# Layer 0's weight conversion in half steps: a spectral layer and two MLPs on one Trainium2 core

## The chip, the cores and the metric

The kernel runs on one core of one Trainium2 chip. The metric is the device time of one execution in microseconds (us), from the first to the last instruction and what lies around them; lower is better.

## What is computed

Two batches of 3008 x 256 go through a real Fourier transform along the sequence, a complex 256 x 256 linear map with a bias and a soft threshold, and the transform back. The 6016 x 256 result passes two MLPs of width 2048, one with a PReLU (`alpha`), one with a quadratic gate. Cut to what matters:

```
X = rfft(x, axis=1)
Yr, Yi = Xr @ w_r - Xi @ w_i + b_r,  Xr @ w_i + Xi @ w_r + b_i
Y = sign(Y) * max(|Y| - 0.01, 0)        (both parts)
x = irfft(Y).reshape(6016, 256)
h = x @ w_in;   x = (max(h,0) + alpha*min(h,0)) @ w_out           # layer 0
h = x @ w_in2;  out = where(h>=1, h, where(h<=-1, 0, (h+1)**2/4)) @ w_out2   # layer 1
```

The MLP weights reach the kernel as float64 words, read as pairs of 32-bit integers; the kernel itself makes an fp32r pair of high and low part from each.

## The kernel before

**Phases.** Phase 1 (`f1`) makes the first factor of the transform. Phase 2 runs over 24 items `(b, i)`, 12 per batch, in passes j = 0 to 23. Pass j emits `f2(j+2)` (second factor for the item two ahead), `mix(j)` (the complex map), `i1(j-2)` (first factor back), from pass 16 on `p3(j-16)` (second factor back, which yields the MLP's input `y`), and then steps of the weight conversion. Passes 22 and 23 have no `f2` left. Behind the loop stand `i1` of item 22, the first MLP block `first(0, 0, 0)`, and `i1` of item 23. Then come the MLPs: 12 chunks of tokens times 16 blocks f of the hidden width for each of two layers. Step i emits `first` of one block and `second` of the block three steps earlier; the first two chunks are interleaved in 32 steps.

**Order.** The schedule is manual: each engine works through its instructions in the order in which the code emits them. SP (SyncE) issues nearly all DMAs, also in that order. So an instruction that waits holds back all that stands behind it on its engine.

**An item of phase 2.** ACT (ScalarE) copies the PSUM of `f2` to the high half `fh` (lines 317, 318), DVE (VectorE) subtracts for the low half `fl` (319), ACT completes it (320); only then can `mix` use the item. Behind `mix`, DVE makes `t`, `clip` and `y` (337 to 339), and `i1` needs `y`. PSUM has four buffers under each of two tags: `mix` and `i1` share "o", all the rest "h".

**The conversion.** Block f of layer 0 is loaded by two DMAs to staging buffer `u` (three of them, taken in turn), and then goes through this sequence; `cm` and `cp` have two buffers each:

- ACT 145 `cm<-u` (absolute value of the top word), ACT 146 `u<-u` (the low word as a float), DVE 147 `cp<-u` (the sign)
- DVE 179 clamp of `cm`, DVE 158 `cm<-cm,cp`, which finishes the value
- ACT 174 `w<-cm`, the high part of the weight; DVE 163 and 164, the fraction of the low word
- DVE 168 `cm<-cm,w` and 169 `w<-cm,cp`, the low part

The generator `conversions` yields after each step. Before, a step is either "163, 164, 174 of block k-1 and 145 to 147 of block k" or "168, 169 of block k-1, then 179, 158 of block k, then the load of block k+2". So a block takes two steps. In passes 5 to 16 one step is taken, in passes 17 to 21 two, in 22 and 23 one; in the interleaved chunks one at each step i that 3 does not divide. Layer 1's first 15 blocks use GpSimd (E is G) and keep their steps.

Of the kernel before, what the change touches and what calls it, by code (L numbers as in the profile page):

```python
# [74 lines left out]
def spectral_mlp_kernel(ctx: ExitStack, tc: tile.TileContext, x, w_r, w_i, bias, c_f1, c_f2,  # L75
# [47 lines left out]
    def in_place(l, f):  # L123
        return l == 1 and f >= 12
# [9 lines left out]
        nc.sync.dma_start(u[:, 256:512, :].rearrange("p m z -> p (m z)"),  # L134
                          w_dram[l][1][f * 128:(f + 1) * 128, :].bitcast(U32))

    def convert_w(l, f, part, clamp, low_engine):
        E = low_engine
        if part == 0:
            u = stage.pop((l, f))  # L140
            m = rot.tile([128, 512], F32, tag="cm", name=f"cm{l}_{f}")
            p = rot.tile([128, 512], F32, tag="cp", name=f"cp{l}_{f}")
            live[l, f] = u, m, p
            top, low = u[:, :, 1], u[:, :, 0]
            A.activation(m, top.bitcast(F32), AF.Abs, scale=2.0 ** -16)
            A.activation(low.bitcast(F32), low, AF.Copy, scale=2.0 ** -52)
            V.tensor_scalar(p.bitcast(U32), top, 0x80000000, 0x80000000, op0=ALU.bitwise_and, op1=ALU.bitwise_xor)
            if clamp is G:
                clamp_w(l, f, G)
            return  # L150
        u, m, p = live[l, f]
        low = u[:, :, 0].bitcast(F32)
        mu, pu = m.bitcast(U32), p.bitcast(U32)
        if part == 1:
            if clamp is V:
                clamp_w(l, f, V)

            V.scalar_tensor_tensor(mu, mu, 3, pu, op0=ALU.logical_shift_left, op1=ALU.bitwise_xor)
        elif part == 2:
            if not in_place(l, f):  # L160
                high_w(l, f, m)

            V.tensor_scalar(pu, mu, 0xFF800000, None, op0=ALU.bitwise_and)
            E.tensor_tensor(p, p, low, op=ALU.mult)
        else:
            if in_place(l, f):
                high_w(l, f, m)
            E.tensor_tensor(m, m, wt[l, f][:, 0, :].bitcast(F32), op=ALU.subtract)
            E.tensor_tensor(wt[l, f][:, 1, :], m, p, op=ALU.add)
            del live[l, f]  # L170

    def high_w(l, f, m):
        wt[l, f] = block(w_tag[l, f], [128, 2, 512], F32R, f"w{l}_{f}")
        A.activation(wt[l, f][:, 0, :], m, AF.Copy)

    def clamp_w(l, f, engine):

        m = live[l, f][1]
        engine.tensor_scalar(m, m, W_MAX, W_MIN, op0=ALU.min, op1=ALU.max)

    def conversions(l, fs, clamp, low_engine):

        n = len(fs)
        for f in fs[:2]:
            load_w(l, f)
            yield
        for k in range(n + 1):
            if k >= 1:
                convert_w(l, fs[k - 1], 2, clamp, low_engine)
            if k < n:  # L190
                convert_w(l, fs[k], 0, clamp, low_engine)
            yield
            if k >= 1:
                convert_w(l, fs[k - 1], 3, clamp, low_engine)
            if k < n:
                convert_w(l, fs[k], 1, clamp, low_engine)
            if k + 2 < n:
                load_w(l, fs[k + 2])
            yield
# [90 lines left out]
    load_a(0, A_PARTS[4:])  # L290
    load_mn(1, n_t, c_i1)
    load_mn(2, m_t, c_f2)
    conv = conversions(0, list(range(NF)), V, V)
    next(conv)
    wm = [block(f"c{k}", [128, 2, 2, D], F32R, f"wm{k}") for k in range(2)]
    for g in range(8, 16):
# [196 lines left out]
    for j in range(n):  # L493
        if 0 < j < n - 2:
            f2(*items[j + 2])
        mix(*items[j])
        if j == 0:
            f2(*items[2])
        if j >= 2:
            i1(*items[j - 2])  # L500

        if j == 3:
            for g in range(8, 16):
                store_a(g, 1)
        if j == 5:
            load_a(1, A_PARTS[:3])
            load_mn(2, n_t, c_i1, 0)
            load_a(1, A_PARTS[3:4])
            load_mn(2, n_t, c_i1, 1)
        if j == 7:  # L510
            load_a(1, A_PARTS[4:])
            nc.sync.dma_start(nalpha, alpha)
            nc.sync.dma_start(g47, c_i2)
        if j == 13:
            for g in range(3):
                load_v(g)
        if j >= P3_AT:
            g = j - P3_AT
            p3(g)
            if g + 3 < 8:  # L520
                load_v(g + 3)
        if j == 20:
            V.tensor_scalar(nalpha, nalpha, -1.0, None, op0=ALU.mult)
        if j == n - 2:
            prep(0, 0)
        for _ in range((j >= 5 or j == 2) + (17 <= j < 22)):
            next(conv)
    i1(*items[n - 2])
    first(0, 0, 0, None)
# [9 lines left out]
    for i in range(len(seq) + DEPTH):  # L539
        if i < len(seq):  # L540
            l, c, f = seq[i]
            if (l, c, f) == (0, 2, 0):
                for _ in conv:
                    pass
                conv = conversions(1, list(range(15)), G, G)
            if (l, c, f) == (0, NC - 1, 4):
                for _ in conv:
                    pass
                conv = conversions(1, [15], V, V)
            if i >= 1:  # L550
                first(l, c, f, seq[i - 1])
            if i == 2:
                prep(0, 1)
            if 8 <= i < 24 and i % 2 == 0:
                p3(4 + i // 2)
            if 3 <= i < 2 * NF and i % 3 != 0 or l == 0 and c >= 2 and f % (2 if c == NC - 1 else 4) == 0:
                next(conv, None)
            if (l, c, f) == (0, 0, NF - 1):
                prep(0, 2)
# [38 lines left out]
```

## Time and profile before

| | |
|---|---|
| median of 3 runs | 1146.31 us (1145.3 to 1146.49) |
| profiled execution | 1149.25 us, span 1147.2 us |
| mean granted TensorE clock | 0.997 |
| PE busy | 1136.1 us, 99% of the span |
| DVE busy | 905.6 us, 79% |
| ACT busy | 630.6 us, 55% |
| phase 2 | about 34 to 154 us of the span |
| MLP layer 0, then 1 | about 155 to 654 us, then to the end |

PE is TensorE's matmul queue. A busy PE is not a PE at its peak, since ends of matmuls are modelled; idle PE time and the granted clock are the safer readings. A wait is named by line and tile: "PE psi L346 <- DVE y L339" is the transform back waiting for the thresholded item.

### The profile page before, as it was taken

The page shows a single profiled execution, that of the slowest core. Times are in us where ns is not written, and L with a number is a line of the kernel's source. Part 1 is how long each engine was busy: PE and PEld are TensorE (multiplying, and loading weights), DVE is VectorE, ACT ScalarE, POOL GpSimd, SP SyncE. Part 2 cuts the span into 40 slices and gives each one's busy share as a digit, 9 for nine tenths or more (in the row PEclk, how much of TensorE's full clock was granted, in tenths as well). Part 3 has the DMA queues.
Part 4 walks back from the last instruction along what each step waited for, and adds up shares of the span by engine and source line. Part 5 has one row for each costly group of instructions (what it writes and reads, how often), then busy time and mean ns, then how long its engine had stood idle before and what let it go on. Part 6 is the DMA issues. An engine that isn't in the chain of part 4 may idle for free.

```text
span 1147.2 us, 17412 instructions
## 1 busy us (share of the span) xinstructions
PE 1136.1 (99%) x6630; PEld 1013.4 (88%) x6630; DVE 905.6 (79%) x1409; ACT 630.6 (55%) x1131; POOL 81.5 (7%) x64
## 2 busy tenths in 40 slices
PE   9999999999999999999999999999999999999998
PEld 6999978888888998888889988888889988888898
DVE  2679977668999999999986777777777777777776
ACT  3455677675655666565555755445445544544553
POOL 0000000000231313212210000000000000000000
PEclk9999999999999999999999999999999999999999
DMA  9997662100010101000000000000000000000000
GB/s 278 323 293 217 183 180 60 57 1 1 20 37 20 37 19 32 25 19 19 1 1 19 1 1 19 19 1 19 19 1 19 17 10 10 20 19 1 19 19 17
DMA packets 38195, 59.40 MB, mean 52 GB/s; under 512 B 3712, under 2 KB 25568, under 8 KB 38112
## 3 DMA queue, kind: packets, MB, share of 16 engines
q1 hardware_dynamic: 37856, 58.14, 16.4%
q8 instruction: 53, 0.87, 0.3%
q14 instruction: 30, 0.25, 0.1%
q10 hardware_dynamic: 256, 0.15, 0.0%
HBM read 39.53 MB, written 18.74 MB: 51 GB/s over the span
## 4 chain that ended last, share of the span: by engine, by line
PE 90%; DVE 4%; DMA 2%; ACT 2%; issue 1%; SPq 0%; DVEq 0%; ACTq 0%
PE pso L95 14%; PE pso L94 14%; PE pso L96 13%; PE psh L94 13%; PE psh L95 13%; PE psh L96 13%; PE psm L332 5%; PE psf L312 2%; PE psi L346 2%; DMA x<-in_x 1%; PE ps L420 1%; DVE gl L91 1%; DVE ta L456 1%; DMA wm<-in_w_r 1%; DMA a_dr<-ae 1%
## 5 line engine op out<-in xcount | busy, mean ns | idle before, releaser
L91 DVE TENSOR_TENSOR gl<-ta,gh 128x512 fp32r<-128x512 f32 (+1 forms) x384 | 274.5, 715 | 50.0 <-ACT gh L88 44.9
L94 PE MATMUL psh<-mxh,w 128*128 128x512 f32 (+1 forms) x768 | 288.9, 376 | 0.7 <-ACT tb L454 0.6
L94 PE MATMUL pso<-gh,w 128*128 128x512 f32 (+1 forms) x768 | 288.5, 376 | 0.0
L95 PE MATMUL psh<-mxl,w 128*128 128x512 f32 (+1 forms) x768 | 288.3, 375 | 0.0
L95 PE MATMUL pso<-gl,w 128*128 128x512 f32 (+1 forms) x768 | 288.0, 375 | 0.2
L96 PE MATMUL psh<-mxh,w 128*128 128x512 f32 (+1 forms) x768 | 288.1, 375 | 0.0
L96 PE MATMUL pso<-gh,w 128*128 128x512 f32 (+1 forms) x768 | 287.7, 375 | 0.0
L461 ACT ACTIVATE ta<-psh 128x512 f32<-128x512 f32 (+1 forms) x192 | 113.6, 592 | 243.5 <-PE psh L96 216.8
L462 DVE SCALAR_TENSOR_TENSOR tb<-ta 128x512 f32<-128x512 f32 (+1 forms) x192 | 130.7, 681 | 116.4 <-ACT ta L461 115.8
L453 ACT ACTIVATE ta<-psh 128x512 f32<-128x512 f32 (+1 forms) x192 | 113.6, 592 | 193.6 <-DVE gl L91 96.6
L456 DVE SCALAR_TENSOR_TENSOR ta<-ta,nalpha,tb 128x512 f32<-128x512 f32 (+1 forms) x192 | 168.0, 875 | 11.9 <-ACT tb L454 11.6
L94 PEld LDWEIGHTS psh<-mxh,w 128*128 128x128 f32 x768 | 145.6, 190 | 18.9 <-ACT tb L454 1.5
L95 PEld LDWEIGHTS psh<-mxl,w 128*128 128x128 f32 x768 | 145.4, 189 | 17.8 <-DVE mxl L91 0.3
L95 PEld LDWEIGHTS pso<-gl,w 128*128 128x128 f32 x768 | 145.1, 189 | 18.1 <-DVE gl L91 1.3
L96 PEld LDWEIGHTS psh<-mxh,w 128*128 128x128 f32 x768 | 145.4, 189 | 17.3
L94 PEld LDWEIGHTS pso<-gh,w 128*128 128x128 f32 x768 | 145.1, 189 | 17.4
L96 PEld LDWEIGHTS pso<-gh,w 128*128 128x128 f32 x768 | 145.2, 189 | 17.2
L88 ACT ACTIVATE gh<-ta 128x512 fp32r<-128x512 f32 (+1 forms) x240 | 147.6, 615 | 1.3 <-DVE ta L464 1.3
L464 DVE TENSOR_TENSOR ta<-psh,tb 128x512 f32<-128x512 f32 (+1 forms) x192 | 129.1, 672 | 0.0
L454 ACT ACTIVATE tb<-psh 128x512 f32<-128x512 f32 (+1 forms) x192 | 112.5, 586 | 0.0
L90 DVE CAST gh<-ta 128x512 fp32r<-128x512 f32 (+1 forms) x144 | 67.1, 466 | 15.2 <-DVE ta L456 0.5
L332 PE MATMUL psm<-wm,fh 128*128 128x256 f32 x384 | 60.6, 280 | 0.0
(54 smaller groups left out, 798.1 us busy)
## 6 DMA issues: line engine op xcount, KB each, us to landing
u<-in_w_in SPq DMA_DIRECT2D x32, 256.0 KB, 2.7
u<-in_w_out SPq DMA_DIRECT2D x32, 256.0 KB, 3.0
v_dr<-ve SPq DMA_DIRECT2D x12, 512.0 KB, 3.1
v<-v_dr SPq DMA_DIRECT2D x32, 192.0 KB, 4.8
x<-in_x SPq DMA_DIRECT2D x15, 384.0 KB, 7.7
out<-yt SPq DMA_DIRECT2D x20, 256.0 KB, 2.0
a<-a_dr SPq DMA_DIRECT2D x6, 768.0 KB, 7.0
a_dr<-ae SPq DMA_DIRECT2D x20, 192.0 KB, 6.6
```

The source lines that it names most:

```text
L88: A.activation(hi, src, AF.Copy)
L91: V.tensor_tensor(lo, src, hi.bitcast(F32), op=ALU.subtract)
L94: T.matmul(ps, wl, xh, start=start, stop=False)
L95: T.matmul(ps, wh, xl, start=False, stop=False)
L96: T.matmul(ps, wh, xh, start=False, stop=stop)
L332: T.matmul(o, x[:, 2 * k + c, off:off + 128], wm[r][:, z, c, :].rearrange("p (h q) -> p q h", h=2), start=n == c == 0, stop=n == 5 and c == 1)
L453: A.activation(ta, ps, AF.Relu, scale=-1.0)
L454: A.activation(tb, ps, AF.Relu)
L456: V.scalar_tensor_tensor(ta, ta, nalpha[:, f:f + 1], tb, op0=ALU.mult, op1=ALU.add)
L461: A.activation(ta, ps, AF.Relu, bias=0.5, scale=0.5)
L462: V.scalar_tensor_tensor(tb, ta, 1.0, ta, op0=ALU.min, op1=ALU.mult)
L464: V.tensor_tensor(ta, ps, tb, op=ALU.max)
```

## The change

The two kinds of step of layer 0 become four: "fraction of block k-1 (174, 163, 164), and 145 of block k", "146 and 147 of block k", "168 and 169 of block k-1", and "179, 158 of block k and the load of block k+2". They are taken twice as often: two in each of passes 5 to 16, four in 17 to 21, none in 22 and 23, one at each step i from 3 in the interleaved chunks. Layer 1's last block, converted beside chunk 11, also takes the small steps, one per block f. No instruction is added or removed.

```diff
--- before.py
+++ after.py
@@ -134,40 +134,39 @@
         nc.sync.dma_start(u[:, 256:512, :].rearrange("p m z -> p (m z)"),
                           w_dram[l][1][f * 128:(f + 1) * 128, :].bitcast(U32))
 
-    def convert_w(l, f, part, clamp, low_engine):
-        E = low_engine
-        if part == 0:
-            u = stage.pop((l, f))
-            m = rot.tile([128, 512], F32, tag="cm", name=f"cm{l}_{f}")
-            p = rot.tile([128, 512], F32, tag="cp", name=f"cp{l}_{f}")
-            live[l, f] = u, m, p
-            top, low = u[:, :, 1], u[:, :, 0]
-            A.activation(m, top.bitcast(F32), AF.Abs, scale=2.0 ** -16)
-            A.activation(low.bitcast(F32), low, AF.Copy, scale=2.0 ** -52)
-            V.tensor_scalar(p.bitcast(U32), top, 0x80000000, 0x80000000, op0=ALU.bitwise_and, op1=ALU.bitwise_xor)
-            if clamp is G:
-                clamp_w(l, f, G)
-            return
+
+    def begin_w(l, f):
+        u = stage.pop((l, f))
+        m = rot.tile([128, 512], F32, tag="cm", name=f"cm{l}_{f}")
+        p = rot.tile([128, 512], F32, tag="cp", name=f"cp{l}_{f}")
+        live[l, f] = u, m, p
+        A.activation(m, u[:, :, 1].bitcast(F32), AF.Abs, scale=2.0 ** -16)
+
+    def words_w(l, f):
         u, m, p = live[l, f]
-        low = u[:, :, 0].bitcast(F32)
-        mu, pu = m.bitcast(U32), p.bitcast(U32)
-        if part == 1:
-            if clamp is V:
-                clamp_w(l, f, V)
-
-            V.scalar_tensor_tensor(mu, mu, 3, pu, op0=ALU.logical_shift_left, op1=ALU.bitwise_xor)
-        elif part == 2:
-            if not in_place(l, f):
-                high_w(l, f, m)
-
-            V.tensor_scalar(pu, mu, 0xFF800000, None, op0=ALU.bitwise_and)
-            E.tensor_tensor(p, p, low, op=ALU.mult)
-        else:
-            if in_place(l, f):
-                high_w(l, f, m)
-            E.tensor_tensor(m, m, wt[l, f][:, 0, :].bitcast(F32), op=ALU.subtract)
-            E.tensor_tensor(wt[l, f][:, 1, :], m, p, op=ALU.add)
-            del live[l, f]
+        top, low = u[:, :, 1], u[:, :, 0]
+        A.activation(low.bitcast(F32), low, AF.Copy, scale=2.0 ** -52)
+        V.tensor_scalar(p.bitcast(U32), top, 0x80000000, 0x80000000, op0=ALU.bitwise_and, op1=ALU.bitwise_xor)
+
+    def sign_w(l, f):
+
+        mu, pu = (t.bitcast(U32) for t in live[l, f][1:])
+        V.scalar_tensor_tensor(mu, mu, 3, pu, op0=ALU.logical_shift_left, op1=ALU.bitwise_xor)
+
+    def fraction_w(l, f, E):
+
+        u, m, p = live[l, f]
+        if not in_place(l, f):
+            high_w(l, f, m)
+        V.tensor_scalar(p.bitcast(U32), m.bitcast(U32), 0xFF800000, None, op0=ALU.bitwise_and)
+        E.tensor_tensor(p, p, u[:, :, 0].bitcast(F32), op=ALU.mult)
+
+    def low_w(l, f, E):
+        u, m, p = live.pop((l, f))
+        if in_place(l, f):
+            high_w(l, f, m)
+        E.tensor_tensor(m, m, wt[l, f][:, 0, :].bitcast(F32), op=ALU.subtract)
+        E.tensor_tensor(wt[l, f][:, 1, :], m, p, op=ALU.add)
 
     def high_w(l, f, m):
         wt[l, f] = block(w_tag[l, f], [128, 2, 512], F32R, f"w{l}_{f}")
@@ -178,7 +177,7 @@
         m = live[l, f][1]
         engine.tensor_scalar(m, m, W_MAX, W_MIN, op0=ALU.min, op1=ALU.max)
 
-    def conversions(l, fs, clamp, low_engine):
+    def conversions(l, fs, E):
 
         n = len(fs)
         for f in fs[:2]:
@@ -186,14 +185,23 @@
             yield
         for k in range(n + 1):
             if k >= 1:
-                convert_w(l, fs[k - 1], 2, clamp, low_engine)
+                fraction_w(l, fs[k - 1], E)
             if k < n:
-                convert_w(l, fs[k], 0, clamp, low_engine)
+                begin_w(l, fs[k])
+                if E is V:
+                    yield
+                words_w(l, fs[k])
+                if E is G:
+                    clamp_w(l, fs[k], G)
             yield
             if k >= 1:
-                convert_w(l, fs[k - 1], 3, clamp, low_engine)
+                low_w(l, fs[k - 1], E)
+                if E is V:
+                    yield
             if k < n:
-                convert_w(l, fs[k], 1, clamp, low_engine)
+                if E is V:
+                    clamp_w(l, fs[k], V)
+                sign_w(l, fs[k])
             if k + 2 < n:
                 load_w(l, fs[k + 2])
             yield
@@ -290,7 +298,7 @@
     load_a(0, A_PARTS[4:])
     load_mn(1, n_t, c_i1)
     load_mn(2, m_t, c_f2)
-    conv = conversions(0, list(range(NF)), V, V)
+    conv = conversions(0, list(range(NF)), V)
     next(conv)
     wm = [block(f"c{k}", [128, 2, 2, D], F32R, f"wm{k}") for k in range(2)]
     for g in range(8, 16):
@@ -523,7 +531,8 @@
             V.tensor_scalar(nalpha, nalpha, -1.0, None, op0=ALU.mult)
         if j == n - 2:
             prep(0, 0)
-        for _ in range((j >= 5 or j == 2) + (17 <= j < 22)):
+
+        for _ in range(j == 2 or (2 if 5 <= j < n - 2 else 0) + (2 if 17 <= j < 22 else 0)):
             next(conv)
     i1(*items[n - 2])
     first(0, 0, 0, None)
@@ -542,18 +551,18 @@
             if (l, c, f) == (0, 2, 0):
                 for _ in conv:
                     pass
-                conv = conversions(1, list(range(15)), G, G)
+                conv = conversions(1, list(range(15)), G)
             if (l, c, f) == (0, NC - 1, 4):
                 for _ in conv:
                     pass
-                conv = conversions(1, [15], V, V)
+                conv = conversions(1, [15], V)
             if i >= 1:
                 first(l, c, f, seq[i - 1])
             if i == 2:
                 prep(0, 1)
             if 8 <= i < 24 and i % 2 == 0:
                 p3(4 + i // 2)
-            if 3 <= i < 2 * NF and i % 3 != 0 or l == 0 and c >= 2 and f % (2 if c == NC - 1 else 4) == 0:
+            if 3 <= i < 2 * NF or l == 0 and c >= 2 and f % (1 if c == NC - 1 else 4) == 0:
                 next(conv, None)
             if (l, c, f) == (0, 0, NF - 1):
                 prep(0, 2)
```

The generator starts with two loads and, for k = 0, with three small steps in place of two large ones. So the pairs fall anew on the passes. Three places follow, with the kernel before ahead of the change; lines in the changed file are 8 higher from 310 on (317 is 325) and 174, 145, 146 are 173, 143, 148; 147, 163, 164, 179, 158 are 149, 161, 162, 178, 154. In names, `fh0_11` is item 11, `fh1_9` is item 12 + 9 = 21, and `cm0_2` is block 2 of layer 0.

ACT around pass 9, before:

```order
L317 ACTIVATE fh0_11_804<-psf0_11_799 128x4x128
L318 ACTIVATE fh0_11_804<-psf0_11_799 128x4x64
L320 ACTIVATE fl0_11_805<-fl0_11_805 128x4x64
L349 ACTIVATE ve0_6_790<-psi0_7_841 128x512
L174 ACTIVATE w0_1_846<-cm0_1_740 128x512
L145 ACTIVATE cm0_2_850<-u0_2_682 128x512
L146 ACTIVATE u0_2_682<-u0_2_682 128x512
L317 ACTIVATE fh1_0_860<-psf1_0_855 128x4x128
```

The same place after the change:

```order
L173 ACTIVATE w0_1_799<-cm0_1_689 128x512
L143 ACTIVATE cm0_2_803<-u0_2_682 128x512
L325 ACTIVATE fh0_11_811<-psf0_11_806 128x4x128
L326 ACTIVATE fh0_11_811<-psf0_11_806 128x4x64
L328 ACTIVATE fl0_11_812<-fl0_11_812 128x4x64
L357 ACTIVATE ve0_6_792<-psi0_7_848 128x512
L148 ACTIVATE u0_2_682<-u0_2_682 128x512
```

The first conversion instruction of block 2 (`cm0_2<-u0_2`) stood behind item 11's `fh` and `i1` copies; it now stands ahead of item 11's `fh`.

DVE in pass 18, from `y` of the item to `fl` of item 21, before:

```order
L339 TENSOR_TENSOR y32_1_6_1428<-t1_6_1427,clip1_6_1426 128x512
L163 TENSOR_SCALAR cp0_6_1379<-cm0_6_1378 128x512
L164 TENSOR_TENSOR cp0_6_1379<-cp0_6_1379,u0_6_1135 128x512
L147 TENSOR_SCALAR cp0_7_1481<-u0_7_1285 128x512
L168 TENSOR_TENSOR cm0_6_1378<-cm0_6_1378,w0_6_1476 128x512
L169 TENSOR_TENSOR w0_6_1476<-cm0_6_1378,cp0_6_1379 128x512
L179 TENSOR_SCALAR cm0_7_1480<-cm0_7_1480 128x512
L158 SCALAR_TENSOR_TENSOR cm0_7_1480<-cm0_7_1480,cp0_7_1481 128x512
L319 TENSOR_TENSOR fl1_9_1498<-psf1_9_1492,fh1_9_1497 128x4x128
```

After the change:

```order
L347 TENSOR_TENSOR y32_1_6_1435<-t1_6_1434,clip1_6_1433 128x512
L149 TENSOR_SCALAR cp0_7_1395<-u0_7_1285 128x512
L168 TENSOR_TENSOR cm0_6_1292<-cm0_6_1292,w0_6_1390 128x512
L169 TENSOR_TENSOR w0_6_1390<-cm0_6_1292,cp0_6_1293 128x512
L178 TENSOR_SCALAR cm0_7_1394<-cm0_7_1394 128x512
L154 SCALAR_TENSOR_TENSOR cm0_7_1394<-cm0_7_1394,cp0_7_1395 128x512
L161 TENSOR_SCALAR cp0_7_1395<-cm0_7_1394 128x512
L162 TENSOR_TENSOR cp0_7_1395<-cp0_7_1395,u0_7_1285 128x512
L327 TENSOR_TENSOR fl1_9_1505<-psf1_9_1499,fh1_9_1504 128x4x128
```

Block 7's `cm0_7<-cm0_7,cp0_7` and its reader `cp0_7<-cm0_7` now stand in one pass, with only the fraction's two instructions between the former and `fl`; before, block 7's fraction came one pass later.

ACT from pass 18 to `fh` of item 21, before:

```order
L174 ACTIVATE w0_6_1476<-cm0_6_1378 128x512
L145 ACTIVATE cm0_7_1480<-u0_7_1285 128x512
L146 ACTIVATE u0_7_1285<-u0_7_1285 128x512
L317 ACTIVATE fh1_9_1497<-psf1_9_1492 128x4x128
L318 ACTIVATE fh1_9_1497<-psf1_9_1492 128x4x64
```

After the change:

```order
L148 ACTIVATE u0_7_1285<-u0_7_1285 128x512
L173 ACTIVATE w0_7_1492<-cm0_7_1394 128x512
L143 ACTIVATE cm0_8_1496<-u0_8_1387 128x512
L325 ACTIVATE fh1_9_1504<-psf1_9_1499 128x4x128
L326 ACTIVATE fh1_9_1504<-psf1_9_1499 128x4x64
```

The high part ahead of item 21's `fh` is block 7's now, not block 6's: it reads the `cm0_7` that DVE finishes in this very pass. The same holds in passes 6, 8, ... 16 and in each of 17 to 21.

## Rows read from the trace of the kernel before

**Rows 1.** Stretches: us, busy of PE, PEld, DVE, ACT, POOL, clock, DMA share

```profile
150.00:160.00 10.00, 7.98 (x29) 6.30 (x29) 7.08 (x12) 4.84 (x10) 0.00 (x0) 0.83 0.45 157
160.00:200.00 40.00, 39.31 (x412) 32.65 (x411) 31.57 (x51) 31.26 (x59) 0.00 (x0) 1.00 0.48 106
200.00:240.00 40.00, 40.00 (x419) 34.33 (x419) 25.43 (x39) 27.76 (x55) 0.00 (x0) 1.00 0.14 41
620.00:650.00 30.00, 30.00 (x160) 29.81 (x159) 20.26 (x34) 22.14 (x43) 0.00 (x0) 1.00 0.06 18
```

**Rows 2.** Waits of the whole span, PE: us in total, times, longest

```profile
PE psi L346 <- DVE y L339: 2.0, 1, 2.0
```

**Rows 3.** Timeline, PE: start us, us, instruction, [idle before, what ended it]

```profile
154.25 1.61 PE L346 MATMUL psi<-y,n 128*128 128x256 f32 x4 [2.02 <-DVE y L339]
```

**Rows 4.** Timeline, DVE: splits of items 11, 15, 16 and 17

```profile
78.61 0.68 DVE L319 TENSOR_TENSOR fl<-psf,fh 128x512 fp32r<-128x512 f32 x1
...
98.69 0.68 DVE L319 TENSOR_TENSOR fl<-psf,fh 128x512 fp32r<-128x512 f32 x1
...
102.76 0.69 DVE L319 TENSOR_TENSOR fl<-psf,fh 128x512 fp32r<-128x512 f32 x1 [0.18 <-ACT fh L318]
...
107.55 0.68 DVE L319 TENSOR_TENSOR fl<-psf,fh 128x512 fp32r<-128x512 f32 x1
```

**Rows 5.** The chain that ended last: start us, us, what; passes 17 and 18

```profile
116.08 1.08 PE ps L420 x64
...
121.79 1.08 PE ps L420 x64
```

**Rows 6.** Timeline, DVE, passes 19 to 21

```profile
131.47 0.42 DVE L163 TENSOR_SCALAR cp<-cm 128x512 uint32<-128x512 uint32 x1
...
132.57 0.42 DVE L147 TENSOR_SCALAR cp<-u 128x512 uint32<-128x512 uint32 x1
...
134.69 0.69 DVE L158 SCALAR_TENSOR_TENSOR cm<-cm,cp 128x512 uint32<-128x512 uint32 x1
135.30 0.69 DVE L319 TENSOR_TENSOR fl<-psf,fh 128x512 fp32r<-128x512 f32 x1
...
141.55 0.68 DVE L319 TENSOR_TENSOR fl<-psf,fh 128x512 fp32r<-128x512 f32 x1
```

**Rows 7.** Timeline, DVE, passes 22 and 23

```profile
147.81 0.68 DVE L337 TENSOR_TENSOR t<-psm,b_t 128x512 f32<-128x512 f32 x1
...
149.60 1.22 DVE L91 TENSOR_TENSOR mxl<-yt,mxh 128x1024 fp32r<-128x1024 f32 x1
...
152.35 0.66 DVE L337 TENSOR_TENSOR t<-psm,b_t 128x512 f32<-128x512 f32 x1
...
153.50 0.69 DVE L339 TENSOR_TENSOR y<-t,clip 128x512 f32<-128x512 f32 x1
```

**Rows 8.** Timeline, ACT, passes 20 to 22

```profile
137.55 0.64 ACT L174 ACTIVATE w<-cm 128x512 fp32r<-128x512 f32 x1
138.07 0.69 ACT L145 ACTIVATE cm<-u 128x512 f32<-128x512 f32 x1
138.66 0.69 ACT L146 ACTIVATE u<-u 128x512 f32<-128x512 uint32 x1
139.24 0.58 ACT L317 ACTIVATE fh<-psf 128x512 fp32r<-128x512 f32 x1
139.72 0.38 ACT L318 ACTIVATE fh<-psf 128x256 fp32r<-128x256 f32 x1
...
145.55 0.63 ACT L349 ACTIVATE ve<-psi 128x512 f32<-128x512 f32 x1
...
146.76 1.11 ACT L88 ACTIVATE mxh<-yt 128x1024 fp32r<-128x1024 f32 x1
```

**Rows 9.** Timeline, SP's queue: second half of block 2's load

```profile
75.95 0.65 SPq L134 DMA_DIRECT2D u<-in_w_out  x1
```

**Rows 10.** Timeline, ACT: first conversion instruction of block 2

```profile
83.01 0.69 ACT L145 ACTIVATE cm<-u 128x512 f32<-128x512 f32 x1 [2.26 <-DMA u<-in_w_out]
```

## The prediction

> **What bounds the kernel now.** The page comes first: PE is busy nearly throughout, so only PE's idle time and a lowered clock can be won back, or added to. The waits of PE over the whole span name one long one, `i1` of the last item waiting 2.0 us for `y` [rows 2]; the timeline puts it at 154.25 us, where phase 2 ends [rows 3]. The stretches show what follows: between 150 and 160 us PE was granted 0.83 of its clock [rows 1], a loss of (1 - 0.83) x 10 = 1.7 us, after which it runs at full speed. Between 160 and 200 us another 0.7 us is idle (39.31 of 40), from 200 us on nothing [rows 1]. So 2.0 + 1.7 + 0.7 = 4.4 us is all that an ideal end of phase 2 could give.
>
> The more important reading is who is late. In phase 2 a pass with `p3` costs PE 121.79 - 116.08 = 5.71 us, 1.08 of it `p3` [rows 5], so one without at most 4.6; and the order of work leaves two passes between an item's `mix` and the `i1` that needs its `y`. DVE's timeline shows how near it is to setting the pace: item 15's `fl` starts at 98.69 and item 17's at 107.55, so two passes take 8.86 us, of which DVE idled 0.18 us ahead of item 16's [rows 4]; the work is 8.68 us in two passes. From pass 17 on, with a whole block per pass, it takes 141.55 - 135.30 = 6.25 us [rows 6], with no idle time, against PE's 5.71. DVE falls behind, and its last `y`, started at 153.50 and 0.69 long, ends at 154.19 [rows 7]: that is the wait in rows 3. Anything that stretches DVE's pass in phase 2 therefore comes out at PE.
>
> **What the change takes away.** No instruction goes. Passes 22 and 23 lose their conversion: between the first chunk's low half `mxl` and `t` of item 23 stood 152.35 - 149.60 - 1.22 = 1.5 us of it [rows 7]. What is deferred (about one block) lies in the interleaved chunks, which get one small step per step i, less per step than before (three small steps for four). Block 15 is then complete at i = 23 and needed at i = 26. I cost this at nothing; the cover is PE's own work, with DVE busy only 25.4 of 40 us from 200 us on [rows 1]. If the cover failed, the present 0.7 us would stay.
>
> Layer 1's last block is converted at five neighbouring blocks of chunk 11. PE had no idle time there (30.00 of 30) with DVE at 20.3 and ACT at 22.1 of 30 [rows 1]; I cost it at nothing, and at most at one 0.6 us ACT instruction.
>
> **What it adds: a hand-round in each pass.** After the change ACT's high part of block k (`w<-cm`) stands in the same pass as DVE's instruction that finishes that `cm`, and ahead of the next item's `fh`. ACT cannot take it until DVE is there, and everything behind it on ACT waits; DVE, two instructions later, waits for that `fh`. From rows: DVE finishes `cm` 0.69 us after its start [rows 6]. ACT then needs 0.52 (137.55 to 138.07) for `w`, 0.59 for the next block's absolute value, 0.48 and 0.38 for the two copies of `fh` [rows 8], and two changes of engine at 0.06 each, the time from `y`'s end at 154.19 to PE's start at 154.25 [rows 3, 7]: 0.69 + 0.52 + 0.59 + 0.48 + 0.38 + 0.12 = 2.78 us. DVE meanwhile has 0.61 of its own spacing (134.69 to 135.30) and 1.10 of fraction (131.47 to 132.57) [rows 6]: 1.71 us. So DVE idles 1.07 us where before it idled 0.18 or not at all. The trace of before shows no such sequence; the bounds are 0.5 (half the chain overlapped) and 1.2 (spacings as long as the slower rows). I take 1.07, since each part has a row.
>
> This happens in the even passes from 6 to 16 and in each of 17 to 21. Two passes then take DVE 8.68 + 1.07 = 9.75 us against PE's 9.2 at most, and a pass from 17 on 6.25 + 1.07 = 7.32 against 5.71. DVE sets the pace, and PE stops for PSUM and for `y`.
>
> **What it moves: block 2 is wanted one pass earlier.** ACT started block 2 at 83.01 after idling 2.26 us for the load [rows 10], whose second half SP issued at 75.95 [rows 9]; nothing before that load in SP's order moves, so it lands when it did. Now this instruction stands ahead of item 11's `fh`. So `fh` starts at 83.01 + 0.59, and `fl` of item 11 at 83.01 + 0.59 + 0.48 + 0.38 + 0.06 = 84.5 instead of 78.61 [rows 4, 8]: DVE is 5.9 us later there, and with 9.75 us to two passes it never wins it back.
>
> A rule of the Trainium skill speaks against just this, "DMA: Bandwidth & Descriptors", section "Rules for kernel authors": issue a load early and wait on it late. [...]
>
> **The sum**, as the end of the last `y`. From 84.5: item 11's `fl` to item 19's, eight passes, 4 x 9.75 = 39.0, so 123.5; to item 23's, four passes, 4 x 7.32 = 29.3, so 152.8; to `t` of item 22 as now, 147.81 - 141.55 = 6.26 [rows 6, 7]; to `mxl` 1.79; a wait for its high half, since ACT does `w`, 0.59, then 1.21 of copies (145.55 to 146.76) and 1.11 of `mxh` [rows 8]: 0.7; `mxl` 1.22; `t` to the end of `y` 1.84 [rows 7]. In all 164.6 against 154.19: +10.4. From there before lost 1.7 to the clock and 0.7 to idle PE. I count both as won, since PE's waits are now spread over the passes and ACT and DVE have less conversion beside the first blocks: +10.4 - 1.7 - 0.7 = +8.0. The profiled execution would go from 1149.25 to 1157.3; it lies 2.9 above the median of the runs, and on that median, 1146.31, the forecast is 1154.3 us.
>
> **Rivals.**
> - *The hand-round, and the clock falls once more.* PE now waits at both `i1` behind the loop and for `mxl`; before, one wait of 2.0 us there was followed by a low clock. Price +1.7: 1156.0. For it: the sum of the waits is larger; against: each is shorter. The Trainium skill, "TensorE: Matmul & The Clock Gate", section "A second HAM failure mode: psum-queue depth-cycling", describes a clock that swings where PE idles briefly and often while buffers cycle. Falls inside the passes would cost little, for DVE sets the pace there.
> - *Hand-round alone.* The load lands before it is wanted. Then item 11's `fl` is later only by the 1.07 us of passes 6 and 8: 80.7, and the same terms end at 160.8: +6.6 - 2.4 = +4.2, 1150.5. Against it: 83.01 is in the trace.
> - *Block 2's wait alone.* ACT's wait for `cm` costs DVE nothing. Then 84.5 + 4 x 8.68 + 4 x 6.25 + 6.26 + 1.79 + 1.22 + 1.84 = 155.3: +1.1, less 0.7, the clock as now: 1146.7.
> - *The change gives what it takes away.* Neither wait costs anything, `y` of item 23 ends 1.5 us earlier, the clock does not fall and 0.7 us of idle goes: 1142.4. It decides from the point where ACT finds `cm` ready, that is where DVE has 1.07 us of other work between finishing `cm` and the next `fl`; the order shows only the fraction there.
>
> **Numbers.** Chances in the order told: forecast 0.52, clock again 0.25, hand-round alone 0.08, block 2 alone 0.08, gain 0.07. A measurement of this kernel tells about 0.2% (2.3 us) from no change. So slower 0.85, same 0.08, faster 0.07. The eight hand-rounds behind item 11's `fl` that stretch DVE's passes are worth 4.6 us less at 0.5 each, 1149.7, and 1.0 more at 1.2, 1155.3, with the clock 1157.0. Range 1149.5 to 1157.0, rounded from these; the two cases below it hold 0.15.
>
> **What would show it.** In the trace after: DVE idle about 1.0 us ahead of `fl`, ended by ACT `fh`, in each of passes 17 to 21 (a period of 7.2 to 7.4 us); ACT waiting some 2 us for DVE ahead of `w<-cm`; ACT idle some 7 us ahead of block 2's first instruction at about 83 us; `p3` and `mix` waiting for PSUM; the last `y` near 164.5 us; no PE idle from 170 us on. The forecast is wrong if `fl`'s period in passes 17 to 21 stays at 6.25, or if the load of block 2 lands well before 83 us.

## The result

The changed kernel took 1155.08 us (median of four runs), the kernel before 1146.4 beside it: a ratio of 1.0074, 95% interval 1.0058 to 1.0090, that is 8.5 us slower (6.6 to 10.3). The forecast was 1154.3, in a range of 1149.5 to 1157.0. The profiled execution took 1155.77 us, its span 1153.8. One execution each of three kernels of the next section ran at a granted clock of 0.56 to 0.75 and took 1486 to 2006 us; their medians and ratios leave it out.

The waits of the changed kernel between 60 and 170 us (engine and instruction that wait, what they wait for: us in total, times, longest):

```profile
ACT w L173 <- DVE cm L154: 21.8, 11, 2.4
ACT fl L328 <- DVE fl L327: 17.8, 17, 1.9
DVE fl L327 <- ACT fh L326: 13.5, 11, 4.7
ACT cm L143 <- DMA u<-in_w_out: 3.7, 1, 3.7
```

The same window in the kernel before has one such row:

```profile
DVE fl L319 <- ACT fh L318: 4.3, 6, 1.6
```

The first and the third row are the two halves of the predicted hand-round: eleven times ACT stands at the high part until DVE has finished `cm`, and DVE stands at `fl` until ACT has got round to `fh`. (Of DVE's eleven waits ten are rounds, since no `fl` follows the last one; the other is 1.39 us at item 8, which the kernel before has too. The longest, 4.7, also holds block 2's wait.) The kernel before waited 4.3 us in all, six times, at that `fl`, and never at the high part. The fourth row is block 2, which is wanted earlier.

One round in the timelines of the changed kernel (start us, us, instruction, [idle before it, what ended it]), first ACT, then DVE; the last row is the next item's `fl`:

```profile
128.25 0.63 ACT L173 ACTIVATE w<-cm 128x512 fp32r<-128x512 f32 x1 [2.28 <-DVE cm L154]
128.79 0.79 ACT L143 ACTIVATE cm<-u 128x512 f32<-128x512 f32 x1
129.49 0.58 ACT L325 ACTIVATE fh<-psf 128x512 fp32r<-128x512 f32 x1
129.96 0.38 ACT L326 ACTIVATE fh<-psf 128x256 fp32r<-128x256 f32 x1
```

```profile
127.53 0.69 DVE L154 SCALAR_TENSOR_TENSOR cm<-cm,cp 128x512 uint32<-128x512 uint32 x1
128.25 0.43 DVE L161 TENSOR_SCALAR cp<-cm 128x512 uint32<-128x512 uint32 x1
128.79 0.82 DVE L162 TENSOR_TENSOR cp<-cp,u 128x512 f32<-128x512 f32 x1
130.37 0.69 DVE L327 TENSOR_TENSOR fl<-psf,fh 128x512 fp32r<-128x512 f32 x1 [0.77 <-ACT fh L326]
...
137.59 0.69 DVE L327 TENSOR_TENSOR fl<-psf,fh 128x512 fp32r<-128x512 f32 x1 [0.76 <-ACT fh L326]
```

Read it as a relay. DVE's `cm` ends at 128.22; ACT starts the high part at 128.25 and comes to the end of `fh` at 130.34; DVE's `fl` starts at 130.37. From the start of `cm` to `fl` are 2.84 us, predicted 2.78; in the kernel before `fl` followed 0.61 us behind [rows 6]. The period, 137.59 - 130.37 = 7.22 us, stood at 6.25.

Block 2, in the timelines of ACT and DVE, where the kernel before had `fl` at 78.61 [rows 4]:

```profile
78.15 0.63 ACT L173 ACTIVATE w<-cm 128x512 fp32r<-128x512 f32 x1 [1.94 <-DVE cm L154]
82.49 0.76 ACT L143 ACTIVATE cm<-u 128x512 f32<-128x512 f32 x1 [3.71 <-DMA u<-in_w_out]
...
83.63 0.38 ACT L326 ACTIVATE fh<-psf 128x256 fp32r<-128x256 f32 x1
84.04 0.69 DVE L327 TENSOR_TENSOR fl<-psf,fh 128x512 fp32r<-128x512 f32 x1 [4.74 <-ACT fh L326]
```

The end of phase 2, on DVE and PE; `psi` of item 23 is the instruction of [rows 3]:

```profile
152.25 0.69 DVE L327 TENSOR_TENSOR fl<-psf,fh 128x512 fp32r<-128x512 f32 x1 [0.78 <-ACT fh L326]
...
163.27 0.69 DVE L347 TENSOR_TENSOR y<-t,clip 128x512 f32<-128x512 f32 x1
...
160.68 1.80 PE L354 MATMUL psi<-y,n 128*128 128x256 f32 x4 [1.72 <-DVE y L347]
...
163.97 0.57 PE L95 MATMUL psh<-mxl,w 128*128 128x512 f32 x1
...
164.60 1.03 PE L354 MATMUL psi<-y,n 128*128 128x256 f32 x4
```

The last `y` ends at 163.27 + 0.69 = 163.96 (predicted 164.6; before 154.19 [rows 7]), and item 23's `psi` starts at 164.60, 10.35 us later than the 154.25 of [rows 3]. Stretches of the changed kernel (us from the start, length, busy of PE, PEld, DVE, ACT, POOL, granted clock, DMA share):

```profile
110.00:133.00 23.00, 21.47 (x367) 19.46 (x365) 19.78 (x36) 14.24 (x31) 0.00 (x0) 1.00 0.79 212
133.00:143.00 10.00, 10.00 (x157) 9.51 (x150) 8.86 (x17) 4.72 (x11) 0.00 (x0) 0.83 0.44 132
...
160.00:170.00 10.00, 9.32 (x36) 7.92 (x37) 5.58 (x8) 6.55 (x13) 0.00 (x0) 0.83 0.30 105
170.00:200.00 30.00, 30.00 (x314) 25.49 (x313) 25.16 (x40) 25.34 (x48) 0.00 (x0) 1.00 0.71 159
```

PE now idles inside phase 2, as an engine that waits on DVE does. Its clock fell to the lower level twice (a mean of 0.83 over 10 us each time, 0.50 from 135 to 137 and from 162 to 164 us), and from 170 to 200 us nothing is idle, against 0.7 us between 160 and 200 before [rows 1].

### The profile page after: what moved, and what is told of

It reads as the page before. It is cut to its first block, busy times and chain, and to the rows that moved or that the text cites. A ratio compares the mean times of both kernels' runs of the same rounds, so it can differ in the third digit from the quotient of the medians.

```text
span 1153.8 us, 17422 instructions
## 1 busy us (share of the span) xinstructions
PE 1140.4 (99%) x6630; PEld 1016.9 (88%) x6630; DVE 907.5 (79%) x1409; ACT 633.2 (55%) x1131; POOL 81.6 (7%) x64
## 4 chain that ended last, share of the span: by engine, by line
PE 88%; DVE 6%; DMA 2%; issue 1%; ACT 1%; SPq 0%; DVEq 0%; ACTq 0%
PE pso L94 14%; PE pso L95 14%; PE pso L96 14%; PE psh L95 14%; PE psh L94 14%; PE psh L96 14%; PE psm L340 3%; PE psf L320 1%; PE psi L354 1%; DVE fl L327 1%; PE ps L428 1%; DVE ta L464 1%; DMA wm<-in_w_r 1%; DMA x<-in_x 1%; DVE t L345 1%
```

## The experiments

The theory: two separate waits make the loss, the hand-round and, less, block 2's early want; passes 22 and 23 give a little back. The main rival: the loss is block 2's alone, or that of the smaller steps themselves (more of them in phase 3, other spacing). The executions come to phase 2 up to 3 us apart, even of kernels alike so far (before, and before with the relief alone: 64.37 and 62.47 us at item 8's `fl`), so I read in each trace the time from the start of item 8's `fl` to that of item 23's `psi`. The kernel before, run beside each of them, had medians of 1145.7 to 1146.4 us. A trace is one execution: those of "high part later" and "before, block 2 early" took 1152.25 and 1149.98 us, 4 us more than their medians, that of "both" 1143.26, 4 us less.

| kernel | median us | ratio to before (95%) | item 8's `fl` | last `psi` | between | item 22's `fl` to item 23's |
|---|---|---|---|---|---|---|
| before, first trace | 1146.4 | 1 | 64.37 | 154.25 | 89.9 | 6.26 |
| before, second trace | - | 1 | 64.78 | 154.06 | 89.3 | 6.32 |
| changed | 1155.08 | 1.0074 (1.0058-1.0090) | 64.59 | 164.60 | 100.0 | 7.33 |
| high part later | 1147.84 | 1.0020 (1.0012-1.0029) | 64.41 | 160.44 | 96.0 | 6.57 |
| block 2 early | 1152.81 | 1.0056 (1.0043-1.0069) | 62.88 | 161.96 | 99.1 | 7.32 |
| both | 1147.19 | 1.0006 (0.9997-1.0015) | 62.70 | 151.96 | 89.3 | 6.64 |
| one half-step less | 1143.96 | 0.9987 (0.9977-0.9997) | 61.93 | 150.24 | 88.3 | 6.32 |
| the same, with two edits | 1143.25 | 0.9974 (0.9963-0.9984) | 63.45 | 152.35 | 88.9 | 6.25 |
| before, block 2 early | 1145.90 | 0.9996 (0.9987-1.0006) | 63.60 | 155.32 | 91.7 | 6.34 |
| before, relief alone | 1144.95 | 0.9983 (0.9974-0.9991) | 62.47 | 150.07 | 87.6 | 6.28 |
| before, hand-round everywhere | 1168.24 | 1.0188 (1.0174-1.0201) | 65.17 | 167.21 | 102.0 | 7.84 |
| before, hand-round in phase 2 | 1159.56 | 1.0119 (1.0105-1.0132) | 62.30 | 163.28 | 101.0 | 7.84 |
| changed, without relief | 1157.33 | 1.0104 (1.0088-1.0119) | 63.02 | 163.48 | 100.5 | 7.33 |

**High part later.** In the changed kernel, `high_w` moves out of `fraction_w` and behind the step's first `yield`.

```diff
-    def fraction_w(l, f, E):
+    def fraction_w(l, f, E, high):
...
-        if not in_place(l, f):
+        if high and not in_place(l, f):
             high_w(l, f, m)
...
-                fraction_w(l, fs[k - 1], E)
+                fraction_w(l, fs[k - 1], E, E is G or k == n)
...
                 if E is V:
                     yield
+                    if k >= 1 and not in_place(l, fs[k - 1]):
+                        high_w(l, fs[k - 1], live[l, fs[k - 1]][1])
                 words_w(l, fs[k])
```

> The changed kernel, but ScalarE's high part of a layer-0 block is written one half-step later, ahead of the next block's words, so that it no longer stands in the queue in the same pass as the sign on VectorE that it waits for. Block 2 is still wanted one pass early. Theory (the hand-round between VectorE and ScalarE is most of the loss): the fl of passes 17 to 21 come 6.25 us apart again instead of 7.3, the pairs of passes 6 to 16 8.7 instead of 9.7, the second psi of the last item (164.60 in the changed kernel, 154.25 in the kernel before) comes near 155.7, and the time is 1155.1 - 8.6 = 1146.5 us (1144 to 1149). Rival 1 (the hand-round is idle time that something else would fill; the conversion's early want of block 2 carries the loss): fl periods hardly change and the time stays at 1152 to 1156. Rival 2 (the wait only moves to the next pass's words): the periods stay at 7.3.

ACT no longer waits at the high part, and 1.0074 falls to 1.0020, 6.2 of the 8.5 us. The periods fall to 6.6, not to 6.25. The reason is in this kernel's timelines, ACT and then DVE:

```profile
130.71 0.64 ACT L173 ACTIVATE w<-cm 128x512 fp32r<-128x512 f32 x1
...
132.84 0.72 ACT L143 ACTIVATE cm<-u 128x512 f32<-128x512 f32 x1 [0.90 <-DVE w L169]
...
133.95 0.38 ACT L328 ACTIVATE fh<-psf 128x256 fp32r<-128x256 f32 x1
...
128.47 0.68 DVE L329 TENSOR_TENSOR fl<-psf,fh 128x512 fp32r<-128x512 f32 x1
...
130.85 0.42 DVE L149 TENSOR_SCALAR cp<-u 128x512 uint32<-128x512 uint32 x1
131.39 0.69 DVE L168 TENSOR_TENSOR cm<-cm,w 128x512 f32<-128x512 f32 x1
...
135.12 0.68 DVE L329 TENSOR_TENSOR fl<-psf,fh 128x512 fp32r<-128x512 f32 x1
```

ACT now comes so early to the next block's absolute value that it waits 0.9 us for DVE's low part, the last reader of that buffer. This wait costs DVE nothing: `fh` is done at 133.95 + 0.38 = 134.33, and `fl` starts at 135.12 without idle time ahead of it. What is longer is DVE's own row of instructions. L168, the first of the low part, reads what the high part writes and starts just behind its end (130.71 + 0.64 = 131.35), 0.54 us behind L149; in the kernel before the same two were 0.34 apart (132.57 to 132.91). The rest is wider spacing, as in the changed kernel (last section). In this execution block 2's load also landed late, and ACT waited for it from 75.59 on:

```profile
85.18 0.66 ACT L143 ACTIVATE cm<-u 128x512 f32<-128x512 f32 x1 [9.59 <-DMA u<-in_w_out]
```

It is the execution 4 us over its median, and its last `psi` came at 160.44 where 155.7 was expected.

**Block 2 early.** In the changed kernel, block 2 is loaded right behind block 1.

```diff
         for f in fs[:2]:
             load_w(l, f)
+            if l == 0 and f == 1:
+                load_w(l, 2)
             yield
...
-            if k + 2 < n:
+            if k + 2 < n and (l, k) != (0, 0):
                 load_w(l, fs[k + 2])
```

> The changed kernel, but the load of weight block 2 is issued together with block 1's, in pass 2. Theory: only ScalarE's wait for that load (3.7 us) and what it holds up goes, the hand-round stays: fl periods 9.7 for a pair and 7.3 in passes 17 to 21 as now, the second psi of the last item near 161.3 instead of 164.60, the time 1155.1 - 3.1 = 1152.0 us (1150.5 to 1153.5). Rival (block 2's wait is where the loss begins and the rest follows from it): the time falls to 1146 to 1148. Second rival (the load is late because the queues are full, not because it was issued late, and pushes other loads back): no gain, 1154 to 1157.

2.1 us came back (1.0074 to 1.0056; the intervals overlap). In the trace ACT waits for DVE and no longer for block 2, but it waits for block 3's load, and `fl` of item 13 behind it:

```profile
77.55 0.63 ACT L173 ACTIVATE w<-cm 128x512 fp32r<-128x512 f32 x1 [1.95 <-DVE cm L154]
78.08 0.68 ACT L143 ACTIVATE cm<-u 128x512 f32<-128x512 f32 x1
...
89.59 0.78 ACT L143 ACTIVATE cm<-u 128x512 f32<-128x512 f32 x1 [1.78 <-DMA u<-in_w_out]
...
91.17 0.69 DVE L329 TENSOR_TENSOR fl<-psf,fh 128x512 fp32r<-128x512 f32 x1 [2.79 <-ACT fh L328]
```

So the early load moved a part of the wait to the next block. The hand-round stayed, at 7.32 us a pass. The rival that puts the loss on this wait is out.

**Both edits.**

> The edits of the two kernels before this one together: the high part one half-step later, and block 2 loaded in pass 2. Theory (two separate causes that add up): the second psi of the last item near 153.7, the time 1155.1 - 10.6 = 1144.5 us (1142 to 1147), a little under the kernel before, since the last two passes of phase 2 carry no conversion. Rival (a third cause in the smaller steps): the time stays 2 us or more above the kernel before, 1148 or more.

The way from `fl` to `psi` came back to 89.3 us, as before, and the ratio to 1.0006: together the two edits undid 7.8 us, where apart they gave 6.2 and 2.1. So the two add, as far as the intervals can tell. The median lies just past the expected range and missed the forecast by 2.7 us, so this run by itself does not exclude a third cause of that size; the next one speaks against it. Some 0.3 us in each of passes 17 to 21 is the longer row of DVE just seen, and ACT waited 3.72 us for block 3's load here. The profiled execution, at 1143.26, was the fastest of its runs, and why the others took some 4 us more no trace shows.

**One half-step less.** The changed kernel, with the pairing of steps shifted by one, so that a block's sign and its high part fall into different passes and block 2 is wanted no earlier, both as before.

```diff
-        for _ in range(j == 2 or (2 if 5 <= j < n - 2 else 0) + (2 if 17 <= j < 22 else 0)):
+        for _ in range(j == 2 or (1 if j == 5 else 2 if 5 < j < n - 2 else 0) + (2 if 17 <= j < 22 else 0)):
```

> The changed kernel with one thing altered: in pass 5 one half-step is taken instead of two. All later half-steps of phase 2 then pair up as the whole steps of the kernel before: a block's sign in one pass and its fraction and high part in the next, and block 2 is wanted no earlier than in the kernel before; passes 22 and 23 still carry no conversion, and chunks 0 and 1 take a half-step at each step. Theory: what is left is the relief of passes 22 and 23 (1.5 us on the path to the last y) and the deferred work beside chunks 0 and 1, which has cover: the second psi of the last item near 152.6 against 154.25 in the kernel before, at most 0.7 us given back where block 15's low part is awaited, the time 1146.4 - 1.6 + 0.7 = 1145.5, with less idle beside the first blocks 1143 to 1146.5 us. Rival (the deferred work costs in phase 3, or the half-steps themselves do): 1147.5 or more, with the stalls beside chunks 0 and 1.

As the theory had it: one missing call in pass 5 turns 8.5 us slower into 1.5 us faster (1.0074 to 0.9987). It undoes both waits at once, so it does not part them. Half-steps as such show no cost: whole steps with the same relief came to 0.9983 (below). Block 15's low part came late, and PE idled 0.62 us for it:

```profile
223.57 0.38 PE L96 MATMUL pso<-gh,w 128*128 128x512 f32 x1
224.56 0.45 PE L94 MATMUL psh<-mxh,w 128*128 128x512 f32 x1 [0.62 <-DVE w L169]
```

**The same, with two edits.** Block 2 early as above, and half-steps in phase 3 from step 2.

```diff
-            if 3 <= i < 2 * NF or l == 0 and c >= 2 and f % (1 if c == NC - 1 else 4) == 0:
+            if 2 <= i < 2 * NF or l == 0 and c >= 2 and f % (1 if c == NC - 1 else 4) == 0:
```

> The kernel with one half-step less in pass 5 (1143.96 us), and two edits more: block 2 is loaded together with block 1 in pass 2, and the half-steps in phase 3 begin at step 2 instead of 3, so that block 15's low part is a half-step earlier (its wait was 0.78 us at 223.57). Theory (each takes away its own wait: 0.8 us there, and what ScalarE's wait for block 2's load costs, about 0.7 us): 1142.5 us (1141.5 to 1143.5). Rival (the earlier load takes its time from the loads that phase 1 waits for, or the load wait has cover): no gain, 1143.5 to 1145, the 0.78 us apart.

0.9974, the fastest kernel of the study, 3.0 us under the kernel before (1.8 to 4.2). With step 2 alone and no early load, below, the ratio was 0.9984 (0.9975 to 0.9993), so neither edit's part can be told by itself. In this kernel's trace PE no longer waits for block 15.

> The kernel with one half-step less in pass 5, and the half-steps in phase 3 begin at step 2 instead of 3, without the early load of block 2. It tells which of the two later edits gave the 0.13 per cent. Theory (block 15's wait of 0.78 us): 0.8 us under the kernel with one half-step less, 0.9980 of the kernel before, about 1144.1; the rest was the load. Rival (the load alone gave it): 0.9987, about 1144.9.

1143.79 us, between the two kernels it was to tell apart, and its interval overlaps both: inconclusive. Only its times were read.

**Before, block 2 early.** The load edit alone, in the kernel before.

> The kernel before, with block 2 loaded together with block 1 in pass 2 and nothing else. It prices the load by itself where no half-steps are. Theory: the load's wait of 2.3 us on ScalarE, of which a pass that alternates with a long one hides a part, goes: the second psi of the last item near 152 against 154.25, the time 1145.7 - 2.0 = 1143.7 us (1142.5 to 1145). Rival (the wait is hidden, or the load only pushes others back): 1145 to 1146.5.

0.9996: nothing, as the rival had it. ACT's wait of 2.26 us [rows 10] had not been hidden in the kernel before, where `fh` of item 12 stood behind it and DVE idled:

```profile
85.04 0.69 DVE L319 TENSOR_TENSOR fl<-psf,fh 128x512 fp32r<-128x512 f32 x1 [1.60 <-ACT fh L318]
```

With the early load that wait is gone, but ACT waits longer for other transfers:

```profile
69.09 0.60 ACT L351 ACTIVATE ve<-psi 128x512 f32<-128x512 f32 x1 [4.35 <-DMA v_dr<-ve]
...
92.66 0.80 ACT L145 ACTIVATE cm<-u 128x512 f32<-128x512 f32 x1 [2.10 <-DMA u<-in_w_out]
```

The first is a store that SP issues behind block 2's load, the second is block 3's load; the kernel before waited 0.90 us and nothing at these places. All four kernels with the early load wait 2.05 to 5.13 us for that store, the nine others at most 2.02. That the edit is worth nothing because it moves the wait is argued from these traces, not tested by a run.

**Before, relief alone.**

```diff
-        for _ in range((j >= 5 or j == 2) + (17 <= j < 22)):
+        for _ in range((5 <= j < n - 2 or j == 2) + (17 <= j < 22)):
```

> The kernel before, with whole steps, but no conversion in passes 22 and 23, the two steps left over being done in phase 3. It has the taken-away part of the change alone. Theory (the relief is worth what the two passes carry on the path to the last y, 1.5 us, and half-steps as such cost nothing): like the kernel with one half-step less in pass 5, 1144.2 us (1143 to 1145.5). Rival (half-steps spread the deferred work better, and whole steps beside the first chunks hold the matmuls back): 1145.5 to 1147.5, with stalls beside chunks 0 and 1.

0.9983: 1.9 us faster. The last `fl` and the last `psi`:

```profile
139.04 0.68 DVE L319 TENSOR_TENSOR fl<-psf,fh 128x512 fp32r<-128x512 f32 x1
...
150.07 1.13 PE L346 MATMUL psi<-y,n 128*128 128x256 f32 x4
```

From the one to the other are 150.07 - 139.04 = 11.03 us against 154.25 - 141.55 = 12.70 in the kernel before: 1.67, where the prediction had 1.5. Whole steps did it as well as half-steps.

**Changed, without relief.** The same question from the other side: `2 if j >= 5` for `2 if 5 <= j < n - 2`.

> The changed kernel with two half-steps in passes 22 and 23 too. It undoes the taken-away part alone. Theory (relief worth 1.5 us on the path to the last y): the last item's second psi near 166 against 164.60, the time 1155.1 + 1.5 = 1156.6 us (1155.8 to 1158). Rival (with the matmuls waiting for the hand-round anyhow, the relief is worth nothing): 1154 to 1155.7.

1157.33 against 1155.08, 2.25 us; the intervals just overlap. From `fl` to `psi` are 163.48 - 150.01 = 13.47 us against 164.60 - 152.25 = 12.35. The path shows the relief in the changed kernel too, 1.12 us of it, hidden in the loss; the times agree, but are not clear of the noise.

**Before, hand-round everywhere.** No half-steps, no earlier want, no relief: only the high part of layer 0's blocks is written right behind the sign.

```diff
             V.scalar_tensor_tensor(mu, mu, 3, pu, op0=ALU.logical_shift_left, op1=ALU.bitwise_xor)
+            if low_engine is V and not in_place(l, f):
+                high_w(l, f, m)
         elif part == 2:
-            if not in_place(l, f):
+            if low_engine is G and not in_place(l, f):
                 high_w(l, f, m)
```

> The kernel before, with whole steps as they are, but ScalarE's high part of a layer-0 block written right behind VectorE's sign, in the same pass, instead of in the next step. No instruction more, no load earlier, passes 22 and 23 as before: only the hand-round that the change brought. Theory (that hand-round is the main cause): VectorE idles ahead of the fl in each pass that has a sign, the periods of passes 17 to 21 grow from 6.25 to between 7.3 and 7.9 us, the pairs of passes 6 to 16 from 8.8 to between 9.7 and 10.4, the second psi of the last item comes 8 to 12.5 us later, and the time is 1154 to 1158 us. Rival (the loss of the change lies in its smaller steps or its early load): within 2 us of the kernel before, 1144 to 1148.

This makes the wait from nothing, and larger than the change did. ACT and DVE in this kernel:

```profile
120.98 0.63 ACT L176 ACTIVATE w<-cm 128x512 fp32r<-128x512 f32 x1 [2.52 <-DVE cm L158]
...
122.41 0.69 DVE L321 TENSOR_TENSOR fl<-psf,fh 128x512 fp32r<-128x512 f32 x1 [1.46 <-ACT fh L320]
...
130.13 0.69 DVE L321 TENSOR_TENSOR fl<-psf,fh 128x512 fp32r<-128x512 f32 x1 [1.46 <-ACT fh L320]
```

The period, 130.13 - 122.41 = 7.72 us, and the last `psi`, 13.0 us late, are within or just past what was expected; the time, 1168.2, is 10 us past it. DVE idles 1.46 us here where the changed kernel had 0.77, because none of its own work stands between the sign and `fl`. The excess lies behind the last `psi`: 1167.29 - 167.21 = 1000.1 us against 1147.2 - 154.25 = 992.95. The waits from 167 to 400 us show PE stopped by phase 3's evacuations on ACT:

```profile
PE psh L94 <- ACT tb L456: 3.7, 3, 2.6
```

**Before, hand-round in phase 2.** The same for blocks 0 to 10 alone (`l == 0 and f <= 10`), to tell whether that excess is the hand-round again, in phase 3, or follows from phase 2's lateness.

> The kernel before with the high part right behind the sign, as in the run that made it slower by 22 us, but for blocks 0 to 10 alone, whose signs lie in passes 6 to 21. Pass 23 and phase 3 are as in the kernel before. In that run the last item's second psi came 13.0 us late and another 7.1 us were lost behind it, where half of the signs and high parts still lay. Theory (the hand-round costs where the sign and the next evacuation stand in one pass, wherever that is, and the 7.1 us are the same thing in phase 3): passes 17 to 21 again 7.7 us apart, the last item's second psi near 165.7 (13.0 less 1.5 for pass 23), little lost behind it, 1146.4 + 11.4 = 1157.8 us (1155.5 to 1160). Rival (what was lost in phase 3 follows from phase 2's lateness, by the clock or late transfers): 1163 or more.

1.0119, 13.6 us slower, in the theory's range; `fl` to `psi` 11.1 us longer (the last `psi` is earlier than expected because this execution came to item 8 2.9 us earlier than that with the hand-round everywhere, from which 165.7 was reckoned); behind it 1154.55 - 163.28 = 991.3 us, no excess. So the excess was the round itself, where phase 3 still converts. One instruction's place in ACT's queue costs more here than the whole change.

**The kernel before, a second trace.**

> The kernel before itself, for a second trace. The first trace, on which the sum was made, is of an execution of 1149.25 us, 2.8 us over the median, with the clock at half from 154.76 on. Theory (the fall of the clock belongs to that execution, not to the kernel): an execution near 1146 us shows no fall at that place, the wait for the last y is shorter than 2.0 us, and the span behind the last psi is near 991 us instead of 993. Rival (the clock falls in every execution): the same fall, and the difference lies before 60 us, in the loads.

An execution of 1147.19 us. PE, and the stretch that had a clock of 0.83 in [rows 1]:

```profile
154.06 1.13 PE L346 MATMUL psi<-y,n 128*128 128x256 f32 x4 [1.60 <-DVE y L339]
...
150.00:160.00 10.00, 8.40 (x46) 7.04 (x39) 8.24 (x14) 5.80 (x12) 0.00 (x0) 1.00 0.51 165
```

The clock did not fall, and behind the last `psi` are 1145.14 - 154.06 = 991.1 us, 1.9 less than in the first trace.

## Why the prediction was right, and where it was off

**The hand-round, right in place and size.** Predicted 9.75 us for two passes and 7.32 for one; the trace has 107.57 - 97.85 = 9.72 and 7.22 to 7.36. Predicted was an idle time of 1.07 us ahead of `fl`; it shows as 0.77, because 0.3 us of the longer period lies in wider spacing of the instructions ahead of it. That this round causes the loss is shown from both sides: taken out, 6.2 us come back; put by itself into the kernel before, it costs 13.6 us.

**Block 2, right in place, worth less.** `fl` of item 11 at 84.04, predicted 84.5; that the load came within 0.5 us of the row of before was in part luck, since eight executions spread over 3.8 us (last section). ACT idled 3.71 us ahead of the block's first instruction where I had expected some 7, since the high part had already waited 1.94. Undone, it gave 2.1 us, not the 3.1 that I expected of that run, and block 3's load then held ACT up. The Trainium skill's rule, issue early and wait late ("DMA: Bandwidth & Descriptors", "Rules for kernel authors"), brought 2.1 us here, not clear of the noise, and nothing in the kernel before (0.9996); the traces add that a load issued earlier can delay another transfer.

**The sum behind the last `y`, right by luck in one term.** Last `y` +9.8 against +10.4. I took 1.7 off for the clock. In the profiled pair something like that happened: behind the last `psi` 992.95 became 989.23 us, -3.7: 1.7 of clock, about 0.7 of idle beside the first blocks; another 0.9 lies behind the last output store, which was issued 3.6 us ahead of the end before (1143.58) and 2.7 after (1151.12); why, and what the 0.4 left over is, I did not find. But the second trace shows that the low clock belonged to an execution of the kernel before, not to every one. Against a median of runs that term had no place: +10.4 - 0.7 would have been 1156.0, also inside the measured interval.

**The clock, the rival that came and cost little.** It did fall again, twice. The first fall, between 133 and 143 us, lay where DVE sets the pace. Of the second only 164.60 - 163.96 = 0.6 us, less the usual 0.06, reached the path: PE was still at half-rate `psh` when the last `y` was done. The rival's price of 1.7 was too high for this trace.

**The relief, right**: 1.5 predicted, 1.67 measured on the path. That the deferred work costs nothing held too: from 170 to 200 us PE was busy 30.00 of 30, and from 170 to 400 us 230.00 of 230.

**Open.** Why the runs with both edits, and those with the later high part, spread over 5 us; and how much of the 0.13% between the kernel with one half-step less and the same with two edits is the load and how much step 2.

## What to carry to other kernels

Engines with in-order queues pay for a dependency by what stands behind it, not by its own length: before splitting or regrouping steps, write down for each pass which instruction of one engine waits for one of the other in the same pass, and what the first engine has queued behind it. Give such a pair a pass of distance; here one step shifted by one turned 0.7% slower into 0.1% faster, with the same instructions. A wait whose followers are not needed yet is free (the 0.90 us in the kernel with the high part later). A load issued earlier can make another transfer later, so look at the waits behind it too. And take a second trace before an event of the first, such as a lowered clock, becomes a term of a sum.

## What had not been expected of the hardware

- The granted clock is not the same in two executions of one kernel. PE's waits of 2.0 us (kernel before, first trace), 1.72 us (changed kernel) and 1.61 us (hand-round in phase 2) stood just ahead of a fall; a wait of 1.60 in the kernel before (second trace) did not, nor did one of 1.78 in the changed kernel without relief, where the next, of 2.11, did.
- A DVE instruction of 0.69 us is followed after 0.61 us by one that does not use its result ([rows 6], 134.69 to 135.30) and after 0.72 by one that does (127.53 to 128.25 in the changed kernel): splitting a sequence can cost 0.1 us where independent work stood between.
- Block 2's load, at the same place of SP's queue, let ACT start 17.0 to 20.8 us behind item 8's `fl` in eight executions in which ACT waited for it; a margin of 2 us is less than that spread.
